# Other idle matmuls at the start, 144 empty instructions among the first products, and a set order of two rings, in a retention and gated feed-forward kernel

## The chip, the cores and the metric

The kernel runs on one core of a Trainium2 chip. The time is that of the device in microseconds (us); the time of an execution is a little longer than the span that the profile shows, since the span reaches only from the first instruction of the program to the last. PE is TensorE's matmul, PEld its weight load, DVE VectorE, ACT ScalarE, POOL GpSimd, SP SyncE, which issues nearly all transfers.

## The reference

```python
# q, k, v: (8, 8, 576, 64); moe_w_gate, moe_w_val: (512, 1536); moe_w_out: (1536, 512)
scores = np.matmul(q, k.transpose(0, 1, 3, 2)) / np.sqrt(D)
gamma = 1.0 - 2.0 ** (-5.0 - np.arange(H))
rel = pos[:, None] - pos[None, :]
Dmat = np.where(rel >= 0, gamma[:, None, None] ** rel, 0.0)
attn = np.matmul(scores * Dmat, v)                       # (8, 8, 576, 64)
x = attn.transpose(0, 2, 1, 3).reshape(4608, 512)
gate = 1.0 / (1.0 + np.exp(-(x @ moe_w_gate)))
out = (gate * (x @ moe_w_val)) @ moe_w_out               # (4608, 512)
```

Inputs and output are float32; the kernel multiplies in bfloat16 and adds up in float32.

## The kernel before

The decay is folded into tables: q and k are multiplied by powers of gamma while they are cast to bfloat16 (`cast_pair`, `cast_qk`). What an earlier piece of a sequence leaves for later ones goes through a running state of 64x64 per head. The 4608 rows of x are worked in columns of a transposed x (`xT`): a lead block of 512, two blocks of 256 (512 and 768), and seven blocks of 512 from 1024 on, whose products use a scheme of seven quarter products in place of eight (`quarter_units`, `quarters`).

The schedule is manual: each engine runs its instructions in the order in which the code issues them, and a wait is set where an instruction needs another's result or its buffer.

The lead part, in the order of PE's queue:

- idle matmuls on a zeroed tile `blank` (L245, ten of 128x512 by `fill_wide`), while the first loads of k and q land;
- for two pairs of row tiles: transposes of k and q (`pair_t`, L454), scores (`pair_qk`, L473), state (`first_st`, L510), the masked scores times v (`pair_intra`, L561), with a few idle matmuls among them (`fill`, `fill_wide`; two `fill_wide(2)` among the first scores and another ahead of the first gate product);
- the gate and value products of the lead block, 512 columns wide: column blocks 0 and 1 by `h_one` (hg, hv, L1263; with `pair_st` of one pair behind the first hv and one behind the second hg), 2 to 7 in twos by `h_two` (L1278), 8 to 11 by `h_both` (L1246). Gate tiles take the ring `qk_psum`, value tiles the ring `ffn_psum`; ACT applies the sigmoid, DVE multiplies. 96 matmuls;
- the out products of the lead block (`op_first`, L1426), 48 matmuls, mixed with the third pair of row tiles.

Then the main loop over `BLOCKS` begins. The two blocks of 256 take `h_units` (L816: h_g, h_v, two column blocks to a bank, DVE multiplies at L821) and `op_units` (L1156), whose out product number nb is put into bank nb of `ffn_psum`. Among these run the steps of the attention: `turn_step` (PE transposes for steps 0, 1 and 7, L591; the other steps' tiles are turned by DMA), scores and products into row tiles (L629, L637), values (L655, L670).

A `Ring` is a list of banks in the order in which they were last taken. A tile without a bank of its own takes the first in the list that is not held, and its bank goes to the end. A row tile of the ring of three always takes bank 2. When the main loop begins, the last takers of `ffn_psum` were op_0_0 (bank 1), op_0_1 (bank 2) and op_0_2 (bank 0), so its list is 1, 2, 0; that of `qk_psum`, where op_0_3 took bank 1 last, is 0, 1. In block 512 the order of `h_units` is h_g, h_v for column blocks 0, 2, 4, 6, 8, 10: twelve tiles.

`space()` puts an empty instruction (`nc.tensor.nop`, L252) into PE's queue as long as the list `owed` says so. Two of the later blocks use it:

```python
SPACES = {2560: 40, 3072: 40}
owed.extend([True, False, False, False] * SPACES.get(t0, 0))
```

PE is one instruction queue: each matmul is issued with a weight load of its own.

Of the kernel before, what the change touches and what calls it, by code (L numbers as in the profile page):

```python
# [16 lines left out]
def kernel(  # L17
# [70 lines left out]
    qk_psum = Ring(qk_banks, 2)  # L88
    ffn_psum = Ring(ffn_banks, 3)
# [140 lines left out]
    def idle_bank():  # L230
        idle.append(ffn_psum.tile([P, 4, P], FP32, tag="ffn", name=f"idle_{len(idle)}"))
# [3 lines left out]
    def fill(n, weights=P, columns=P):  # L235

        for i in range(n):
            nc.tensor.matmul(idle[-1][:weights, 0, :columns], lhsT=blank[:, :weights], rhs=blank[:, :columns], start=True, stop=True)

    def fill_wide(n):  # L240

        for _ in range(n):
            nc.tensor.matmul(idle[-1], lhsT=blank, rhs=blank.unsqueeze(1).to_broadcast([P, 4, P]), start=True, stop=True)

    fill_wide(10)  # L245

    SPACES = {2560: 40, 3072: 40}
    owed = []

    def space():  # L250
        if owed and owed.pop():
            nc.tensor.nop(hint="space")  # L252
# [119 lines left out]
    def xT(rows_, cols):  # L372

        t0, n = max(b for b in [(0, 512)] + BLOCKS if b[0] <= cols.start)
        assert cols.stop <= t0 + n
        if t0 not in x_tiles:
            x_tiles[t0] = x_pool.tile([P, M, 512], BF16, tag="x", name=f"xT_{t0}")
        return x_tiles[t0][:, rows_, cols.start - t0:cols.stop - t0]
# [22 lines left out]
    def cast_pair(nm, A, g, eng):  # L401

        if (nm, A) not in natural:
            natural[nm, A] = osb.tile([P, 2, H, D], BF16, tag="osb", name=f"{nm}p_{A}")
        if nm != "v" and A == 2:
            o = natural[nm, A].rearrange("p r (m y) d -> p y m r d", y=2)[:, g]
        else:
            o = natural[nm, A][:, :, g * M:(g + 1) * M, :].rearrange("p r h d -> p h r d")
        i = parts.pop((nm, "pair", A, g))
        if nm == "v":  # L410
            eng(out=o, in_=i)
        else:
            tab = (ktab2 if nm == "k" else qtab2)[:, PAIRS[A][1], g * M:(g + 1) * M, :].unsqueeze(3).to_broadcast([P, M, 2, D])
            eng.tensor_tensor(out=o, in0=i, in1=tab, op=ALU.mult)
# [409 lines left out]
    def gv_unit(t0, u):  # L824

        return gv_pool.tile([P, 4, 512], BF16, tag="gv", name=f"gv_{t0}_{u}")
# [3 lines left out]
    def gv_tile(gvs, t0, fc):  # L830

        if fc not in gvs:
            unit = made[t0, fc // 4] = gv_unit(t0, fc // 4)
            for i in range(4):
                gvs[fc // 4 * 4 + i] = unit[:, i]
        return gvs[fc]
# [63 lines left out]
    def quarter_units(gvs, t0):  # L900
# [44 lines left out]
        of = {}  # L945
        owed.extend([True, False, False, False] * SPACES.get(t0, 0))

# [282 lines left out]
    def last_step(t1):  # L1230
        return max(s for s in range(NS) if at_col[s] < t1)
# [3 lines left out]
    def turn(nm, A, g, pool=ffn_psum, tag="ffn"):  # L1235
        pair_t(nm, A, g, pool, tag, on_act)

    def h_both(fcs):

        for what in ("g", "v"):  # L1240
            for fc in fcs:
                gv = gv_tile(gvs, 0, fc)
                pool, tag = (qk_psum, "qk") if what == "g" else (ffn_psum, "ffn")
                ps = pool.tile([P, 512], FP32, tag=tag, name=f"h{what}_0_{fc}")
                for kc in range(NKC):
                    nc.tensor.matmul(ps, lhsT=(wg_sb if what == "g" else wv_sb)[:, kc, fc * P:(fc + 1) * P],  # L1246
                                     rhs=xT(kc, slice(0, 4 * P)), start=(kc == 0), stop=(kc == NKC - 1))
                if what == "g":
                    nc.scalar.activation(out=gv, in_=ps, func=AF.Sigmoid)
                else:  # L1250
                    nc.vector.tensor_tensor(out=gv, in0=gv, in1=ps, op=ALU.mult)
                yield
# [5 lines left out]
    def h_one(what, fc):  # L1258

        pool, tag = (qk_psum, "qk") if what == "g" else (ffn_psum, "ffn")  # L1260
        ps = pool.tile([P, 512], FP32, tag=tag, name=f"h{what}_0_{fc}")
        for kc in range(NKC):
            nc.tensor.matmul(ps, lhsT=(wg_sb if what == "g" else wv_sb)[:, kc, fc * P:(fc + 1) * P],  # L1263
                             rhs=xT(kc, slice(0, 4 * P)), start=(kc == 0), stop=(kc == NKC - 1))
        gv = gv_tile(gvs, 0, fc)
        if what == "g":
            nc.scalar.activation(out=gv, in_=ps, func=AF.Sigmoid)
        else:
            nc.vector.tensor_tensor(out=gv, in0=gv, in1=ps, op=ALU.mult)

    def h_two(what, f):

        pool, tag = (qk_psum, "qk") if what == "g" else (ffn_psum, "ffn")
        ps = [pool.tile([P, 512], FP32, tag=tag, name=f"h{what}_0_{f + j}") for j in range(2)]
        for i in range(2):
            for j in range(2):
                for kc in (2 * i, 2 * i + 1):
                    nc.tensor.matmul(ps[j], lhsT=(wg_sb if what == "g" else wv_sb)[:, kc, (f + j) * P:(f + j + 1) * P],  # L1278
                                     rhs=xT(kc, slice(0, 4 * P)), start=(kc == 0), stop=(kc == NKC - 1))
        for j in range(2):  # L1280
            gv = gv_tile(gvs, 0, f + j)
            if what == "g":
                nc.scalar.activation(out=gv, in_=ps[j], func=AF.Sigmoid)
            else:
                nc.vector.tensor_tensor(out=gv, in0=gv, in1=ps[j], op=ALU.mult)
# [22 lines left out]
    cast_pair("q", 0, 0, nc.vector)  # L1308
    turn("k", 0, 0, *TR)
    turn("q", 0, 0, *PV)  # L1310
    fill_wide(2)
    cast_pair("q", 0, 1, nc.vector)
    pair_qk(0, 0, QK)
    turn("k", 0, 1, *TR)
    fill(3)
    turn("q", 0, 1, *PV)
    fill_wide(2)
    cast_pair("q", 1, 0, nc.vector)
    pair_qk(0, 1, FF)
    turn("k", 1, 0, *TR)  # L1320
# [34 lines left out]
    pair_out(1, 1, on_act, on_dve)  # L1355
    idle_bank()
    fill_wide(2)
    h_one("g", 0)
    h_one("v", 0)
    pair_st(0, ST)  # L1360
    h_one("g", 1)
    pair_st(1, TR)
    h_one("v", 1)
# [59 lines left out]
    def op_first(fcs, nbs, opps):  # L1423
        for fc in fcs:
            for nb in nbs:
                nc.tensor.matmul(opps[nb], lhsT=gvs[fc][:, nb * P:(nb + 1) * P], rhs=wo_sb[:, fc, :],  # L1426
                                 start=(fc == 0), stop=(fc == NFC - 1))

    opps = [ffn_psum.tile([P, 512], FP32, tag="ffn", name=f"op_0_{nb}") for nb in range(3)]
    op_first((0, 1), range(2), opps)  # L1430
# [59 lines left out]
    pieces = 0  # L1490
    slots = 0
    valued = -1
    for w, (t0, n) in enumerate(BLOCKS):
        nxt = BLOCKS[w + 1] if w + 1 < len(BLOCKS) else None
        last = last_step(nxt[0] + nxt[1]) if nxt else NS - 1
        early = list(EARLY[w]) if w < len(EARLY) else []
        n_h = NFC if n <= 256 else 2 * NFC
        if n == 512:
            n_h = 0
        twos = []  # L1500
        at = slots
        while not early and (not twos and valued < last or twos and twos[-1][0][-1] < last):
            vals = list(range((twos[-1][0][-1] if twos else valued) + 1, at))
            twos.append((vals, list(range(at, min(at + 2, NS)))))
            at = min(at + 2, NS)
        for i, cols in enumerate(ffn_units(t0, n, nxt)):
            if i in SUMS_AT.get(w, ()) and weight_sums:
                weight_sums.pop(0)()
            for step, turn_at in TURN_AT:
                if turn_at == (w, i):  # L1510
                    turn_step(step)
            for x in SPARE.get((w, i - n_h if w == 1 else i), ()):
                x()
            pieces += 1
            if w == 2 and i in (24, 32):
                keeps[0] -= 1
                leave()
            if stores and (nxt is None or w + 2 == len(BLOCKS) and pieces % 4 == 0):
                leave()
            if n > 256 and i % 2 and i < n_h:  # L1520
                continue
            if pending:
                pending.pop(0)()
            elif early:
                if i >= early[0][0]:
                    _, vals, news = early.pop(0)
                    next_two(vals, news, False)
                    valued, slots = ([valued] + vals)[-1], news[-1] + 1
            elif twos and cue:
                cue.clear()  # L1530
                next_two(*twos[0], True)
                valued = twos[0][0][-1]
                slots = max([slots] + [s + 1 for s in twos.pop(0)[1]])
        assert not twos and not early
        while pending:
            pending.pop(0)()
# [31 lines left out]
```

## Time and profile before

| | |
|---|---|
| median of 3 runs | 308.21 us (307.74 to 308.53) |
| the profiled execution | 308.12 us, span 306.4 us |
| PE, PEld busy | 296.4 us (97%), 238.6 us (78%) |
| DVE, POOL, ACT busy | 244.9 us, 209.2 us, 194.9 us |
| PE instructions | 4427 matmuls, 4427 weight loads, 80 empty ones |
| lead block of 512 (to about 54 us), blocks 512 and 768 (to 93.0 us) | 54 us, 39 us |
| a block of 512 from 1024 on | 30.2 us |

In a row of the waits stand who waited and for whom, the sum in us, how often, and the longest. A row of the chain in order of time has start, length and what ran; "issue" is time for which the profile shows no cause. A row of the timeline has start, length, engine, line, operation, out<-in, shape and count, and in brackets the idle time of the engine before it with what ended it; the matmuls of a row overlap, so its length is that of the last one's modelled end. A row of a stretch has its limits and length, then for PE, PEld, DVE, ACT and POOL the busy us and, in brackets, the number of instructions, then the clock granted to PE, the DMA share and GB/s.

### The profile page before, as it was taken

The page shows a single profiled execution, that of the slowest core. Times are in us where ns is not written, and L with a number is a line of the kernel's source. Part 1 is how long each engine was busy: PE and PEld are TensorE (multiplying, and loading weights), DVE is VectorE, ACT ScalarE, POOL GpSimd, SP SyncE. Part 2 cuts the span into 40 slices and gives each one's busy share as a digit, 9 for nine tenths or more (in the row PEclk, how much of TensorE's full clock was granted, in tenths as well). Part 3 has the DMA queues.
Part 4 walks back from the last instruction along what each step waited for, and adds up shares of the span by engine and source line. Part 5 has one row for each costly group of instructions (what it writes and reads, how often), then busy time and mean ns, then how long its engine had stood idle before and what let it go on. Part 6 is the DMA issues. An engine that isn't in the chain of part 4 may idle for free.

```text
span 306.4 us, 10818 instructions
## 1 busy us (share of the span) xinstructions
PE 296.4 (97%) x4427; PEld 238.6 (78%) x4427; DVE 244.9 (80%) x464; ACT 194.9 (64%) x414; POOL 209.2 (68%) x256
## 2 busy tenths in 40 slices
PE   7889999989999999999999999999999999999994
PEld 3644445866868888888888888888888888888883
DVE  5837877887898899689978997898789968945793
ACT  6634744425548757874897479757965886648640
POOL 5875653644467689869976997699769916751670
PEclk9999999999999999999999999999999999999999
DMA  7999999799999992998899948992980390012004
GB/s 208 343 373 403 347 284 214 178 194 193 195 209 213 243 242 52 230 262 181 169 189 226 183 97 204 219 211 63 189 221 4 93 250 8 2 57 84 2 2 137
DMA packets 145730, 54.98 MB, mean 179 GB/s; under 512 B 124048, under 2 KB 138640, under 8 KB 145680
## 3 DMA queue, kind: packets, MB, share of 16 engines
q1 hardware_dynamic: 144880, 53.63, 73.2%
q8 instruction: 35, 0.57, 0.8%
q10 hardware_dynamic: 800, 0.66, 0.7%
q14 instruction: 15, 0.12, 0.1%
HBM read 37.75 MB, written 9.44 MB: 154 GB/s over the span
## 4 chain that ended last, share of the span: by engine, by line
PE 88%; DVE 5%; issue 2%; ACT 2%; DMA 1%; POOL 0%; SPq 0%; DVEq 0%
PE gatea L940 12%; PE wa L940 12%; PE qa L1054 11%; PE qe L1054 9%; PE gatee L940 6%; PE we L940 6%; PE gateg L940 3%; PE op L1156 3%; PE wg L940 3%; PE op L1426 3%; PE h_v L816 2%; PE h_g L816 2%; PE val L655 2%; PE hv L1278 2%; PE hg L1278 2%
## 5 line engine op out<-in xcount | busy, mean ns | idle before, releaser
L427 POOL TENSOR_TENSOR qk<-k,ktab 128x512 bf16<-128x512 f32 x30 | 32.0, 1067 | 9.5 <-DMA k<-in_k_dram 8.0
L1054 PEld LDWEIGHTS <-gsum 128*128 128x128 bf16 x336 | 31.9, 98 | 5.0 <-DVE gsum L877 0.8
L877 POOL TENSOR_TENSOR gsum<-gv 128x256 bf16<-128x256 bf16 (+1 forms) x35 | 26.5, 765 | 13.2 <-DVE gv L965 12.0
L427 POOL TENSOR_TENSOR qk<-q,qtab 128x512 bf16<-128x512 f32 x28 | 30.9, 1102 | 3.6 <-DMA q<-in_q_dram 3.6
L940 PEld LDWEIGHTS <-wg_sb 128*128 128x128 bf16 x308 | 30.1, 98 | 3.7
L940 PEld LDWEIGHTS <-wv_sb 128*128 128x128 bf16 x308 | 30.1, 98 | 3.5
L940 PEld LDWEIGHTS <-wvt 128*128 128x128 bf16 x280 | 27.4, 98 | 3.3
L940 PEld LDWEIGHTS <-wgt_sb 128*128 128x128 bf16 x252 | 24.7, 98 | 2.9
L965 POOL TENSOR_TENSOR gv<-gv,wu 128x512 bf16<-128x512 bf16 x7 | 8.1, 1162 | 26.4 <-DVE wu L991 26.4
L877 POOL TENSOR_TENSOR gsum<-gv,gsum 128x256 bf16<-128x256 bf16 x37 | 25.4, 716 | 0.0
L1054 PEld LDWEIGHTS <-gv 128*128 128x128 bf16 x240 | 23.0, 98 | 3.0
L644 DVE TENSOR_TENSOR pt<-row,tri 128x256 bf16<-128x256 f32 x60 | 21.2, 412 | 4.0 <-PE row L637 3.4
L715 ACT CAST xT<-val 128x256 bf16<-128x256 f32 x60 | 18.9, 388 | 5.9 <-PE val L670 5.9
L432 POOL CAST v<-v 128x512 bf16<-128x512 f32 x20 | 13.7, 683 | 11.9 <-DMA v<-in_v_dram 10.1
L606 ACT CAST sb<-s 128x256 bf16<-128x256 f32 x46 | 17.9, 416 | 5.3 <-DVE s L742 3.1
L940 PE MATMUL wa<-xsum,wv_sb 128*128 128x256 bf16 x140 | 21.0, 273 | 0.0
L940 PE MATMUL gatea<-xsum,wg_sb 128*128 128x256 bf16 x140 | 19.9, 273 | 0.0
L965 POOL TENSOR_TENSOR gv<-gv,ws 128x512 bf16<-128x512 bf16 x15 | 17.5, 1165 | 2.9 <-DVE ws L994 2.9
L994 DVE TENSOR_TENSOR gs<-gatea,gs 128x512 f32<-128x512 f32 x21 | 13.9, 688 | 6.0 <-PE gatea L940 5.2
L994 DVE TENSOR_TENSOR ws<-wa,ws 128x512 f32<-128x512 f32 x21 | 14.4, 685 | 4.2 <-PE wa L940 4.1
L963 ACT ACTIVATE gv<-gs 128x512 bf16<-128x512 f32 x21 | 13.0, 630 | 7.0 <-DVE gs L994 7.0
L986 DVE TENSOR_TENSOR gatee<-gatea,gs 128x512 f32<-128x512 f32 x14 | 9.8, 699 | 9.0 <-PE gatea L940 6.3
(191 smaller groups left out, 857.3 us busy)
## 6 DMA issues: line engine op xcount, KB each, us to landing
k<-in_k_dram SPq DMA_DIRECT2D x26, 256.0 KB, 4.3
q<-in_q_dram SPq DMA_DIRECT2D x26, 256.0 KB, 4.4
v<-in_v_dram SPq DMA_DIRECT2D x26, 256.0 KB, 4.3
out_dram<-ob SPq DMA_DIRECT2D x25, 256.0 KB, 3.1
wg<-in_moe_w_gate_dram SPq DMA_DIRECT2D x12, 256.0 KB, 5.4
wv<-in_moe_w_val_dram SPq DMA_DIRECT2D x12, 256.0 KB, 5.4
wo<-in_moe_w_out_dram SPq DMA_DIRECT2D x12, 256.0 KB, 5.1
v32p<-in_v_dram SPq DMA_DIRECT2D x6, 256.0 KB, 4.5
```

What stands on the lines that cost most here:

```text
L427: eng.tensor_tensor(out=natural_qk[s][:, i].rearrange("p m (y d) -> p y m d", y=2), in0=by_halves(loaded[s][1 - i]), in1=tab, op=ALU.mult)
L432: eng(out=natural["v", s], in_=loaded[s][2])
L606: eng(out=state[key], in_=src)
L644: nc.vector.tensor_tensor(out=probs[s][:, y], in0=row_ps[s][y][:, 0], in1=tri.unsqueeze(1).to_broadcast([P, M, 64]), op=ALU.mult)
L715: nc.scalar.copy(out=x_out(ALL, cols_of(s, i)), in_=x_in(val_ps[s][i], cols_of(s, i)))
L816: nc.tensor.matmul(ps[:, i], lhsT=w_sb[:, kc, (fc + i) * P:(fc + i + 1) * P], rhs=xT(kc, slice(t0, t0 + n)), start=(kc == 0), stop=(kc == ...
L877: eng.tensor_tensor(out=to, in0=a, in1=b, op=op)
L940: nc.tensor.matmul(ps[:, f], lhsT=w[:, kc, f * P:(f + 1) * P], rhs=x[:, kc], start=(first and f == 0 and kc == 0), stop=(f == 1 and kc == ...
L963: nc.scalar.activation(out=to, in_=src, func=AF.Sigmoid)
L965: eng.tensor_tensor(out=to, in0=to, in1=src, op=ALU.mult)
L994: nc.vector.tensor_tensor(out=me["s5"], in0=a, in1=me["s5"], op=ALU.add)
L1054: nc.tensor.matmul(ps[:, b], lhsT=left(fp)[:, b * P:(b + 1) * P], rhs=right(fp), start=(first and fp == 0 and b == 0), stop=(fp == NFC // ...
```

## The change

The ten wide idle matmuls at the start become 56 of 64 columns, and the two `fill_wide(2)` among the first scores become seven of 128 columns each. Counted with their weight loads, these are 112 instructions more, all ahead of the masked scores. `owed` gets 144 entries ahead of the first `h_one`, and `space()` is called behind each matmul of `h_one`, `h_two`, `h_both` and `op_first`: 144 empty instructions, one for each of these 96 and 48 matmuls. Ahead of the main loop both rings are given an order: 0, 1, 2 for `ffn_psum` and 1, 0 for `qk_psum`.

```diff
-    fill_wide(10)
+    fill(56, columns=64)

     SPACES = {2560: 40, 3072: 40}
+    SPACES_FIRST = 144
...
                 for kc in range(NKC):
                     nc.tensor.matmul(ps, lhsT=(wg_sb if what == "g" else wv_sb)[:, kc, fc * P:(fc + 1) * P],
                                      rhs=xT(kc, slice(0, 4 * P)), start=(kc == 0), stop=(kc == NKC - 1))
+                    space()
...
     turn("q", 0, 0, *PV)
-    fill_wide(2)
+    fill(7)
     cast_pair("q", 0, 1, nc.vector)
...
     turn("q", 0, 1, *PV)
-    fill_wide(2)
+    fill(7)
     cast_pair("q", 1, 0, nc.vector)
...
     idle_bank()
     fill_wide(2)
+    owed.extend([True] * SPACES_FIRST)
     h_one("g", 0)
...
                 nc.tensor.matmul(opps[nb], lhsT=gvs[fc][:, nb * P:(nb + 1) * P], rhs=wo_sb[:, fc, :],
                                  start=(fc == 0), stop=(fc == NFC - 1))
+                space()
...
     valued = -1
+    ffn_psum.order = [0, 1, 2]
+    qk_psum.order = [1, 0]
     for w, (t0, n) in enumerate(BLOCKS):
```

The same `space()` stands in `h_one` and `h_two`. `fill(n, weights, columns)` issues n matmuls of `blank` by `blank` with that many columns into an idle bank; `fill_wide(n)` issues n of 512 columns.

More of the change, by code (lines that the diff above doesn't have):

```diff
@@ L1279, in h_two @@
                                      rhs=xT(kc, slice(0, 4 * P)), start=(kc == 0), stop=(kc == NKC - 1))
+                    space()
         for j in range(2):
@@ L1427, in op_first @@
                                  start=(fc == 0), stop=(fc == NFC - 1))
+                space()
     opps = [ffn_psum.tile([P, 512], FP32, tag="ffn", name=f"op_0_{nb}") for nb in range(3)]
```

## The prediction

> **What bounds the kernel now.** I read the page's head, then who waited for whom on PE, then the chain in order of time, and last the counts of instructions in single stretches.
>
> ```profile
> span 306.4 us, 10818 instructions
> PE 296.4 (97%) x4427; PEld 238.6 (78%) x4427; DVE 244.9 (80%) x464; ACT 194.9 (64%) x414; POOL 209.2 (68%) x256
> q8 instruction: 35, 0.57, 0.8%
> PE 88%; DVE 5%; issue 2%; ACT 2%; DMA 1%; POOL 0%; SPq 0%; DVEq 0%
> ```
> ```profile
> PE qkp L473 <- ACT qT L464: 1.3, 4, 0.4
> PE pvp L561 <- issue: 1.1, 1, 1.1
> PE op L1156 <- DVE gv L821: 0.8, 1, 0.8
> ```
>
> TensorE bounds the kernel: 97% busy, 88% of the chain. So a change that leaves the matrix products alone can gain only where PE stands still. Two single waits are large: 1.1 us at L561 for which the profile names no releaser, and 0.8 us at L1156 for a gate-value product on DVE. The rest of PE's waits are at the start, for ACT, DVE and POOL, and no wait of PE is for a DMA. The line of queue q8 is the clue to the first wait: 0.57 MB in 35 packets is 16.3 KB each, and PE's 8,854 shown instructions and 80 empty ones over 35 packets are 255 apiece. So q8 brings PE's own code in blocks of (I take) 256.
>
> **The first wait, and the 112 instructions ahead of it.** The chain, then the counts:
>
> ```profile
> 15.00 0.19 PE pvp L561 x11
> 15.19 1.11 issue
> 16.30 0.41 PE pvp L561 x8
> 17.67 1.02 PE hg L1263 x4
> 20.90 0.37 PE st_None L497 x16
> 21.27 0.97 PE hv L1263 x4
> 22.24 1.73 PE hg L1278 x8
> ```
> ```profile
> 0.00:7.70 7.70, 5.83 (x43) 2.55 (x43) 4.04 (x22) 4.77 (x10) 4.25 (x14) 1.00 0.73 208
> 0.00:11.33 11.33, 8.55 (x96) 4.45 (x96) 7.01 (x26) 7.56 (x14) 7.43 (x17) 1.00 0.86 252
> 0.00:13.82 13.82, 10.69 (x167) 6.21 (x168) 8.89 (x29) 8.85 (x17) 9.59 (x21) 1.00 0.91 269
> 0.00:15.10 15.10, 11.97 (x223) 7.45 (x223) 10.17 (x31) 9.32 (x18) 10.70 (x22) 1.00 0.93 275
> 16.29:21.19 4.90, 4.78 (x66) 2.35 (x66) 1.75 (x3) 1.22 (x3) 4.20 (x9) 1.00 1.09 381
> ```
>
> The wait lies inside one run of equal matmuls (x11, then x8) whose operands and bank the first of them had already, so nothing but the next instruction can be missing. It comes after 223 weight loads and 223 matmuls, 446 instructions. Read as a block's end, the end before is at 446 - 256 = 190, which PE passes at 11.33 (96 + 96). If passing one end asks for the block behind the next, the code took from 11.33 to 16.30: 5.0 us.
>
> Every matmul stands with its own weight load. 56 narrow idle matmuls for 10 wide ones add 92 instructions, twice 7 for 2 add 20: 112, all ahead of both points. So block ends move back by 112. The first falls after 334 old instructions (13.82; 167 + 168), the one before at 190 - 102 = 88 (7.7, 43 + 43; the last 10 of the 112 are not yet passed there). Code asked for at 7.7 is there at 12.7 by the 5.0 us, and needed at 13.8: no wait, 1.1 us to spare. That takes 1.11 off. The next thing late would be the operands of hg and hv, and they are in time: the weights that POOL casts last for the four single products are ready at 17.78, and hv that uses them comes at 21.27 - 1.1 = 20.2.
>
> ```profile
> 17.17 0.61 POOL L311 CAST wv_sb<-wv 128x512 bf16<-128x512 f32 x1
> ```
>
> **The empty instructions and the new second end.** One empty instruction stands behind each of the 96 first gate and value matmuls and the 48 first out products: 144. Before hv of the second column block, the old count is 446 + 132 (the stretch 16.29 to 21.19) = 578. New it is 578 + 112 + 12 empty = 702 = 446 + 256. So the second block end falls exactly ahead of the hv at 21.27, now 20.2. Its code is asked for at 13.82. By 5.0 us it is there at 18.8, 1.4 before need. But DMA moves 381 GB/s there against 275 before, and if a fetch stretches with that, 5.0 x 381 / 275 = 6.9 us: there at 20.7, 0.5 late. I take 0.25, between the two; the ends are 0 and 1.1 (a wait that gives the whole gain back). From there on PE streams 512-wide products, 256 instructions of which (with a third of them empty) last over 18 us, so no later end can be late in this part. And 112 + 144 is 256: behind the last first out product, every block end lies where it lies now, so the rest of the program should neither gain nor lose by it.
>
> What an empty instruction costs can be read from the blocks that have 40 of them already, the third and fourth of these stretches:
>
> ```profile
> L252 PEldq NOP  x80: 13/13/13, 183.2 to 230.0; - x80
> ```
> ```profile
> 93.00:123.19 30.19, 30.19 (x490) 26.74 (x489) 26.64 (x50) 21.41 (x46) 24.46 (x29) 1.00 0.81 185
> 153.51:183.80 30.29, 30.29 (x507) 26.91 (x505) 26.26 (x50) 22.66 (x50) 25.27 (x30) 1.00 0.84 176
> 183.80:213.96 30.16, 30.16 (x490) 26.73 (x489) 25.74 (x48) 22.53 (x49) 25.19 (x30) 1.00 0.86 176
> 213.96:244.18 30.22, 30.22 (x506) 26.92 (x505) 26.38 (x50) 22.82 (x50) 25.30 (x30) 1.00 0.54 117
> ```
>
> Stretches of 490 matmuls: 30.19 without, 30.16 with. Of 506 and 507: 30.22 with, 30.29 without. So 0 us for one in four 256-wide matmuls. Here it is one for each, but each matmul is 512 wide and lasts 0.216 us (1.73 / 8), against 13 ns on the sequencer. I take 0; the other end is 144 x 13 ns = 1.9 us, if nothing covered them.
>
> **The idle matmuls themselves.**
>
> ```profile
> 1.05 3.65 PE L243 MATMUL idle<-blank 128*128 128x512 bf16 x10 [1.05 <-DVE blank L226]
> 4.78 0.40 PE L454 MATMUL kTp<-ident,kp 128*128 128x128 bf16 x4
> 11.33 0.40 PE L238 MATMUL idle<-blank 128*128 128x128 bf16 x4
> ```
> ```profile
> 3.16 0.15 PEld L243 LDWEIGHTS <-blank 128*128 128x128 bf16 x1 [0.28 <-issue]
> 3.59 0.15 PEld L243 LDWEIGHTS <-blank 128*128 128x128 bf16 x1 [0.27 <-issue]
> ```
>
> A wide one takes 0.43 us up to 3.59, so by width a 64-wide one takes 0.054, and 56 take 3.0: done at 4.1, ahead of the first transpose at 4.78. The other bound is the weight load: four 128-wide ones last 0.40 with a fixed part of some 0.2, or 0.06 each later on, hence 0.12 at the early pace; 22 up to 3.7 and 34 at 0.06 end at 5.7, and delay the first transpose by 0.9. Taken: 0, since the width sets the pace in the nearest row. The two sevens are 7 x 0.06 = 0.4 us for 2 x 0.216 = 0.43, under the waits for ACT qT: 0.
>
> **The rings.** Now the ring of three stands at 1, 2, 0 when the main loop begins, and the twelve products of block 512 take the banks in turn, so the last value product sits in bank 0, which the first out product names. It must wait until DVE has read it:
>
> ```profile
> 64.77 0.68 DVE L821 TENSOR_TENSOR gv<-gv,h_v 128x512 bf16<-128x512 bf16 x1
> 65.97 0.69 DVE L821 TENSOR_TENSOR gv<-gv,h_v 128x512 bf16<-128x512 bf16 x1 [0.51 <-PE h_v L816]
> 91.41 0.42 DVE L742 TENSOR_TENSOR s<-s,row 128x256 f32<-128x256 f32 x1
> ```
> ```profile
> 66.70 1.89 PE L1156 MATMUL op<-wo_sb,gv 128*128 128x512 bf16 x8 [0.85 <-DVE gv L821]
> 69.92 3.63 PE L1156 MATMUL op<-wo_sb,gv 128*128 128x512 bf16 x16
> ```
> ```profile
> 93.00 0.87 PE gatea L940 x8
> ```
>
> Starting at 0, 1, 2 the last one sits in bank 2, and bank 0 holds the value product before the last but one, read by 65.45. So the out product starts behind the h_v before it: 0.85 less. What is late next: columns 10 and 11 of the same out product need the value written by 66.66, and they come in the group of 16 at 69.92 - 0.85; the row tile in bank 2 comes with the scores just ahead of that group. Both have over 2 us. The ring is back in the old order after the second out product. The ring of two only swaps the two row tiles, and the first to notice is the second gate product behind 93.00, whose bank is then read until 91.83 instead of some 0.4 sooner: still 1.6 us early. Bounds 0 and 0.85; I take 0.85, since PE has no other wait until the end that a shift brings nearer: loads and casts are ahead of it.
>
> ```profile
> 80.37 1.04 POOL L427 TENSOR_TENSOR qk<-q,qtab 128x512 bf16<-128x512 f32 x1 [0.54 <-DMA q<-in_q_dram]
> ```
> ```profile
> 85.83 0.61 PE L591 MATMUL turn<-ident,qk 128*128 128x128 bf16 x8
> ```
>
> This cast, the nearest that I found, is done 4.4 us before PE turns its tile, more than the two gains together.
>
> **Sum.** -1.11 + 0.25 - 0.85 = -1.7 us. The profiled execution took 308.12 us around its span of 306.4, so 306.4, and its time lies 0.09 under the median of the runs shown (308.21). Forecast: 306.5.
>
> **Rivals.**
> (1) The wait moves: the code for the second end, asked for in the busiest stretch of DMA, comes a microsecond late, so that only the ring's 0.85 is left: 307.4. For it speaks the 381 GB/s, against it the 1.4 us to spare by the one fetch that can be timed.
> (2) The 1.11 us is not code, so it stays, whatever is ahead of it: 307.4 as well. Against it: equal matmuls on both sides, and no releaser. [...]
> (3) The ring's wait comes back at the next DVE step, so only the 0.85 is lost as a gain: 307.3 with my 0.25, 307.0 without.
> (4) Slower: the empty instructions keep weight loads from running ahead. A weight load is 0.098 us here, under a 0.216 us product; exposed behind each of the 144 it would be 14 us, 320. It decides from 12 ns each (1.7 / 144) against any gain, from 18 ns (2.6 / 144) as a loss beyond 0.9 us. Against it stand the two blocks with 40.
>
> ```profile
> L940 PEld LDWEIGHTS <-wg_sb 128*128 128x128 bf16 x308 | 30.1, 98 | 3.7
> ```
>
> **How the numbers follow.** About 0.3% (0.9 us) is what a measurement here can tell from no change, so faster is under 307.3. Forecast 0.57 (306.1 to 307.0); (1) 0.15, (2) 0.06, (3) 0.10, (4) 0.07, and 0.05 for the idle matmuls ending late or rousing PE less, up to 309. Faster: 0.57, 0.09 of (3) and 0.03 of (1): 0.69. Slower: (4) and 0.02: 0.09. Same: 0.22. The range reaches down to the full 1.96 with 0.4 of scatter, up past (1) and (2): 305.9 to 307.7.
>
> **What would show it.** Right: no gap of 1.1 us among the L561 products; hg of the first block near 16.6 instead of 17.67; hv of the second without an "issue" gap over 0.3 ahead of it; eight hg L1278 still 1.73; the L1156 wait gone; q8 with 36 packets; blocks from 93 on as long as now, each about 1.7 earlier. Wrong: an "issue" gap that has only moved to another place of the first 21 us; 512-wide products over 0.216; or the first transposes later than 4.8.

## The result, and the profile after

Over ten runs each the changed kernel took 306.72 us (305.45 to 307.5) and the kernel before 308.25 (307.33 to 311.05): ratio 0.9938 [0.991, 0.9966]. On another chip it was 307.22 against 308.28, ratio 0.9957 [0.9933, 0.9981]. The gain is some 1.1 to 1.5 us. The profiled execution of the changed kernel took 306.89 us, its span is 1.2 us shorter than before.

The head of the page after, with the share of the chain by engine last:

```profile
span 305.2 us, 11063 instructions
PE 296.5 (97%) x4473; PEld 242.7 (80%) x4483; DVE 240.1 (79%) x464; ACT 195.0 (64%) x414; POOL 208.4 (68%) x256
q8 instruction: 36, 0.59, 0.8%
PE 93%; ACT 2%; DVE 1%; issue 1%; POOL 0%; ACTq 0%; POOLq 0%
```

PE's busy time is the same (the trace has no record of 10 of its 4,483 matmuls), its share of the chain went from 88% to 93%: PE waits less. Of PE's waits behind its first matmul these are the largest for an engine and the largest without a releaser (columns: who waited and for whom, us in all, how often, the longest):

```profile
PE kTp L455 <- POOL kp L415: 0.7, 1, 0.7
PE row L638 <- issue: 0.3, 1, 0.3
```

The 1.1 us at the masked scores (now L562) and the 0.8 us at the first out product of block 512 (now L1157) are gone. The chain in order of time, at the places that the prediction named:

```profile
15.69 0.22 PE pvp L562 x8
15.92 0.42 PE pvp L562 x19
...
17.30 0.38 PE hg L1265
...
20.53 0.37 PE st_None L498 x16
20.91 0.97 PE hv L1265 x4
...
23.60 1.73 PE hv L1281 x8
...
65.16 0.35 PE op L1157
...
91.08 0.87 PE gatea L941 x8
...
202.79 0.28 issue
```

The masked scores run through. That the wait before was for code can be seen in the packed trace (the records of which the views are made), which has the time of each packet of q8: the packet of that block ended at 14.88, and PE went on 1.42 us later, at 16.30. After, the packets of the first two blocks ended at 10.98 and 17.18, and PE came to the two ends only at 14.75 and 20.91. The hv at the new second block end (20.91) starts where the state products end (20.53 + 0.37), so nothing waits there. Eight products with an empty instruction behind each still take 1.73 us. But the first hg starts at 17.30, not near 16.6: only 0.37 earlier than before. What went against it stands in the timeline of the start:

```profile
1.05 3.17 PE L238 MATMUL idle<-blank 128*128 128x64 bf16 x56 [1.05 <-DVE blank L226]
4.89 0.61 PE L455 MATMUL kTp<-ident,kp 128*128 128x128 bf16 x4 [0.67 <-POOL kp L415]
5.84 0.95 PE L238 MATMUL idle<-blank 128*128 128x128 bf16 x7
7.59 0.61 PE L455 MATMUL kTp<-ident,kp 128*128 128x128 bf16 x4
10.20 0.40 PE L455 MATMUL kTp<-ident,kp 128*128 128x128 bf16 x4
12.26 0.40 PE L238 MATMUL idle<-blank 128*128 128x128 bf16 x4
41.29 0.39 PE L455 MATMUL qTp<-ident,qp 128*128 128x128 bf16 x4
```

The 56 narrow matmuls end at 4.2, as the width said, and nothing is late because of that: the first transposes start at 4.89, behind the 4.8 that the prediction named as a sign of being wrong, but they wait for POOL's cast. But four transposes take 0.61 us at 4.89 and again at 7.59, and 0.40 only from 10.20 on; before, they took 0.40 from 4.78 on. PE runs at its slow pace some 6 us longer. The four idle matmuls that stood at 11.33 start at 12.26, 0.93 later. (The granted clock in the rows of stretches reads 1.00 for the start in both traces. The packed trace tells more: its record of full clock begins at 3.76 us before and at 9.98 after, where the pace of equal work changes too.)

Against that stand two places at which the trace after is ahead though no part of the change aimed at them. The trace before has these rows, the first in the timeline, the second in the chain:

```profile
41.98 0.40 PE L454 MATMUL qTp<-ident,qp 128*128 128x128 bf16 x4 [0.16 <-DVE qp L414]
88.06 0.34 DVE T L593
```

There PE waited for DVE's cast of q at 41.98 and for DVE's copy of turned tiles at 88.06, and lost some 0.3 us at each. In the trace after DVE is in time at both. That is no gain of the change: the first wait, 0.16 again, is also in the traces of the rings alone and of the 40 empty instructions (below), and not in most of the others; the second is in none of the other thirteen traces, those included that stand behind at 88 us. So it belongs to the one execution before that was profiled.

The lead over the trace before, added up along PE's queue: 0.37 at the first hg (1.11 less 0.74 that the slower start costs), 0.69 at the transposes of q (41.98 to 41.29), 1.54 at the first out product of block 512 (66.70 to 65.16), 1.92 at the first gate product of the main blocks (93.00 to 91.08), and 1.2 at the end. So 0.7 us is given back behind 93 us. Most of that goes at one place, shown here by the timeline before and then after:

```profile
204.21 0.32 PE L637 MATMUL row<-v,qk 64*64 64x64 bf16 x16
204.59 1.48 PE L1054 MATMUL qe<-wo_sb,gv 128*128 128x256 bf16 x12
```
```profile
202.54 0.25 PE L638 MATMUL row<-v,qk 64*64 64x64 bf16 x6
203.41 1.48 PE L1055 MATMUL qe<-wo_sb,gv 128*128 128x256 bf16 x12
```

The lead is 1.67 at the row products and 1.18 behind them, with the issue wait of 202.79 between. That wait stands behind 3,073 weight loads, as many matmuls and 184 empty instructions, 6,330: 5,884 behind the 446 of the first wait, four short of 23 times 256. The code packet ended at 201.59, 1.48 before PE went on at 203.07. So it is a block's end.

### The profile page after: what moved, and what is told of

The parts are those of the page before. It is cut to its first block, busy times and chain, and to the rows that moved or that the text cites. A ratio compares the mean times of both kernels' runs of the same rounds, so it can differ in the third digit from the quotient of the medians.

```text
span 305.2 us, 11063 instructions
## 1 busy us (share of the span) xinstructions
PE 296.5 (97%) x4473; PEld 242.7 (80%) x4483; DVE 240.1 (79%) x464; ACT 195.0 (64%) x414; POOL 208.4 (68%) x256
## 4 chain that ended last, share of the span: by engine, by line
PE 93%; ACT 2%; DVE 1%; issue 1%; POOL 0%; ACTq 0%; POOLq 0%
PE gatea L941 12%; PE wa L941 12%; PE qa L1055 11%; PE qe L1055 9%; PE gatee L941 6%; PE we L941 6%; PE h_v L817 4%; PE h_g L817 3%; PE op L1157 3%; PE op L1431 3%; PE gateg L941 3%; PE wg L941 3%; PE val L656 2%; PE hv L1281 2%; PE hg L1281 2%; PE row L630 2%
## 5 line engine op out<-in xcount | busy, mean ns | idle before, releaser
L428 POOL TENSOR_TENSOR qk<-q,qtab 128x512 bf16<-128x512 f32 x28 | 30.0, 1073 | 4.2 <-DMA q<-in_q_dram 4.2
```

What stands on the lines that cost most here:

```text
L428: eng.tensor_tensor(out=natural_qk[s][:, i].rearrange("p m (y d) -> p y m d", y=2), in0=by_halves(loaded[s][1 - i]), in1=tab, op=ALU.mult)
```

## The experiments

The theory after the result: T1, the 1.11 us was PE's code, and the instructions ahead cured it; T2, the ring order gave its 0.85; T3, the narrow idle matmuls cost 0.7 to 0.9 through the clock; T4, the 144 cost nothing. Each kernel ran beside the kernel before. Ratios are to it.

**The rings alone**, in the kernel before:

```diff
+    ffn_psum.order = [0, 1, 2]
+    qk_psum.order = [1, 0]
```

> The kernel before with the new order of the two rings and nothing else. If the wait at the first out product of block 512 is for bank 0: that wait (0.85 us) goes, the 1.1 us gap in the lead part stays, the first hg stays at 17.7, the time falls by 0.9 to 1.2 us (the trace of the changed kernel has some 0.4 more between 75 and 90, where DVE leads). If the wait only comes back at the next DVE step: no change.

Measured: 307.37 us (306.31 to 308.19) against 308.14, ratio 0.9979 [0.9962, 0.9997], span 305.6. The waits no longer hold the first out product of block 512. They still hold this, at the old place:

```profile
PE pvp L561 <- issue: 0.5, 1, 0.5
```

The chain has the first gate product of the main blocks at 91.27 (93.00 before), though the span is only 0.8 shorter. Of that lead 0.5 goes at a wait for DVE:

```profile
105.60 0.60 PE L940 MATMUL gatee<-xsum,wgt_sb 128*128 128x256 bf16 x4 [0.36 <-DVE gv L965]
```

So the ring order is worth 0.8 us by itself in the medians, as T2 has it, and does not touch the other wait, whose size varies from one execution to another (1.1 and 0.5). Here PE came to the block's end at 15.48, 0.29 later than before, and the packet had ended at 14.71; PE went on at 16.03, 1.32 later.

**All but the rings**: the changed kernel without these two lines.

> The changed kernel without the order of the rings. Theory: the lead part gains 0.4 us up to the first hg (1.1 from the code wait, less 0.7 for a slow clock) and 0.3 more by the out products, so 0.3 to 0.8 us less than before, and the 0.85 us wait at the first out product of block 512 is back. Rival: the lead part's gain is lost behind it, no change.

Measured: 308.03 us (306.54 to 309.41), ratio 0.9988 [0.9964, 1.0012], span 307.5. The wait at the out product is back, and here the clock came later still:

```profile
PE kTp L455 <- POOL kp L415: 1.7, 2, 1.0
PE op L1157 <- DVE gv L822: 0.8, 1, 0.8
```
```profile
11.24 0.61 PE L455 MATMUL kTp<-ident,kp 128*128 128x128 bf16 x4
```

Four transposes still take 0.61 at 11.24. So the idle matmuls and the empty ones together, whose part of the forecast was -1.11 + 0.25, bring nothing that can be told from zero. In this trace what the code wait gave went into a later start, the slow pace and POOL's casts together. That fits T3 and does not show it: the profiled execution (309.22) is among the longer ones of this kernel.

**Wide idle matmuls again, with empty instructions in place of the narrow ones**, so that all counts stay as in the changed kernel:

```diff
-    fill(56, columns=64)
+    for _ in range(10):
+        fill_wide(1)
+        for _ in range(9):
+            nc.tensor.nop(hint="space")
+    for _ in range(2):
+        nc.tensor.nop(hint="space")
...
-    fill(7)
+    fill_wide(2)
+    for _ in range(10):
+        nc.tensor.nop(hint="space")
```

(The last twice, for both groups of seven.)

> The changed kernel with the wide idle matmuls of before, and 112 empty instructions in place of the narrow matmuls, so that every code block ends where it ends in the changed kernel. Theory (narrow idle matmuls do not raise PE's clock in time): four transposes take 0.40 us from the start on as before, not 0.61; the first hg starts at 16.6 instead of 17.3; 0.5 to 0.8 us less than the changed kernel. Rival (the clock's rise is a matter of chance, whatever the idle matmuls): 0.40 or 0.61 by chance, same time as the changed kernel on average. Rival 2 (112 empty ones cost more than they hide): the wide matmuls are stretched beyond 4.7.

Measured: 309.18 us (308.89 to 309.93), ratio 1.0038 [1.0016, 1.0059], so slower than before. The timeline of the start, then of the weight loads:

```profile
1.05 6.69 PE L243 MATMUL idle<-blank 128*128 128x512 bf16 x10 [1.05 <-DVE blank L226]
7.96 0.58 PE L460 MATMUL kTp<-ident,kp 128*128 128x128 bf16 x4 [0.21 <-issue]
1.70 0.11 PEld L243 LDWEIGHTS <-blank 128*128 128x128 bf16 x1 [0.55 <-issue]
```

With nine empties between them the wide ones start 0.65 us apart instead of 0.43, ten take 6.69 us, and the first transposes move from 4.78 to 7.96. Nine empties and two instructions in 0.65 us are some 0.06 us each on average, not the 13 ns that the profile shows for one. So the run did not isolate the width: it made a new bound, and idle work with gaps in it did not raise the clock by 7.96 either (0.58 for four). As a test of the width it is a miss.

**40 empty instructions behind the ten wide idle matmuls, nothing else**, in the kernel before:

```diff
     fill_wide(10)
+    for _ in range(40):
+        nc.tensor.nop(hint="space")
```

> The kernel before with 40 empty instructions behind the ten wide idle matmuls and nothing else. If the 1.1 us gap is a block of code that is late: the gap begins 40 instructions earlier, after 203 weight loads and 203 matmuls instead of 223 each, and is 0.3 to 1.1 us long. If it belongs to the matmul at L561: it stays behind 223 and 223.

Measured in one run: 306.79 us, span 305.1. The wait at the out product stays (0.8). The timeline and the chain:

```profile
1.05 4.45 PE L243 MATMUL idle<-blank 128*128 128x512 bf16 x10 [1.05 <-DVE blank L226]
```
```profile
15.16 0.42 PE pvp L563 x19
16.55 0.59 PE hg L1265 x2
```

No issue wait is left among the masked scores, and hg starts at 16.55, which is the 1.1 us that the prediction wanted. That is neither of the two things expected: the gap has not moved 40 instructions forward, it is gone. An empty instruction takes 13 ns in the trace before, waits for nothing there and nothing waits for it; what the 40 change is the place in the code at which the blocks end. The block's packet ended at 12.25 here, 2.6 us sooner than before, and PE came to that end at 14.75. That speaks against the rival by which the wait is not code; the next run settles it.

**8 empty instructions at the same place.**

```diff
     fill_wide(10)
+    for _ in range(8):
+        nc.tensor.nop(hint="space")
```

> The kernel before with 8 empty instructions behind the ten wide idle matmuls and nothing else. If the 1.1 us gap is a late block of code: it begins 8 instructions earlier, after 219 weight loads and 219 matmuls, 0.4 to 1.1 us long (40 of them made it go, since the fetch is asked for sooner too). If it belongs to the matmul at L561: it stays behind 223 and 223, or is gone.

Measured in one run: 308.15 us, span 306.4. The waits, and the stretch from the start to where PE stands:

```profile
PE val L657 <- issue: 0.5, 1, 0.5
PE pvp L563 <- issue: 0.3, 1, 0.3
```
```profile
0.00:15.98 15.98, 13.09 (x219) 8.10 (x219) 10.29 (x31) 9.52 (x19) 10.67 (x22) 1.00 0.92 265
```

219 matmuls and 219 loads, 438, and the 8 empties are 446: the count at which the wait stood before (223 and 223). So it moved by four matmuls in the work, as a block's end does. It also shrank to 0.3; a second one of 0.5 came in the first of the seven main blocks, 11 times 256 instructions (less two) behind the first. The place follows from the count. The size does not follow from eight instructions by the prediction's 5.0 us. It follows from the packet: that ended at 14.78 here, much as in the trace before (14.88) and with the rings alone (14.71), and PE went on 1.3 to 1.5 us after it in all three (16.23, 16.30, 16.03), but came to the end later, at 15.98, and so waited less. The same holds for all seven such waits of 0.25 us or more in these traces: PE goes on 1.31 to 1.48 us behind the end of a packet on q8. That leaves nothing of the rival.

**The changed kernel without the 144.**

```diff
-    SPACES_FIRST = 144
+    SPACES_FIRST = 0
```

> The changed kernel without the 144 empty instructions among the first products: code blocks end 112 instructions earlier than before through the whole program. If the 144 matter by what they bring back into place: new gaps after 60 us, 0.5 us or more above the changed kernel. If they neither cost nor bring anything: the same time as the changed kernel within 0.3 us.

Measured: 309.89 us (307.87 to 311.06), ratio 1.0055 [1.0035, 1.0076]: 1.6 us over the kernel before, where the changed kernel lies 1.1 to 1.5 under it. So the 144 are worth some 3 us. The chain has two large waits without a releaser:

```profile
117.72 0.16 PE row L630 x16
117.88 0.11 PE val L671 x13
117.99 0.89 issue
149.97 1.22 issue
```

And the stretch from the end of the first to the start of the second, with the stretch behind it, up to the next gap, a small one:

```profile
118.87:149.97 31.10, 31.09 (x512) 27.42 (x512) 25.10 (x49) 22.18 (x50) 25.19 (x30) 1.00 0.91 205
151.18:182.37 31.19, 31.18 (x511) 27.64 (x512) 25.87 (x49) 22.28 (x50) 24.87 (x29) 1.00 0.88 171
```

512 weight loads and 512 matmuls are 1,024 instructions, four times 256, in both stretches (one matmul of the second has no record). This is the plainest sight of code blocks in these traces. The two packets ended at 117.57 and 149.78, and PE went on at 118.88 and 151.19. Without the 144, all ends of the main loop stand 112 instructions earlier in the work, and two of them fall into or just behind a run of short matmuls (16 in 0.16 us), where PE comes to the end sooner than the next block does. The 144 bring the shift to 256 and the ends to where they were.

**80 narrow idle matmuls in place of 56**, in the changed kernel:

```diff
-    fill(56, columns=64)
+    fill(80, columns=64)
```

> The changed kernel with 80 narrow idle matmuls at the start instead of 56, so that they last as long as the ten wide ones (about 4.3 us instead of 3.2). If PE's clock stays low because the narrow ones end too early: four transposes take 0.40 us from the first or second group on, and the first hg starts at 16.6 to 17.0. If it stays low because they are narrow: 0.61 us for the first four groups as in the changed kernel, first hg at 17.3 or later.

Measured in one run: 305.95 us, span 304.2.

```profile
1.05 4.45 PE L238 MATMUL idle<-blank 128*128 128x64 bf16 x80 [1.05 <-DVE blank L226]
5.31 0.61 PE L455 MATMUL kTp<-ident,kp 128*128 128x128 bf16 x4
7.66 0.40 PE L455 MATMUL kTp<-ident,kp 128*128 128x128 bf16 x4
```

The second group of transposes is fast at 7.66, where it was slow at 7.59 with 56. The width is the same, so the width alone did not keep the clock low: with 4.45 us of narrow idle matmuls full clock is on record from 6.04 us, with the 3.17 us of the changed kernel from 9.98. The first hg is hardly earlier, though (17.26): later transposes of k now wait 0.8 for POOL's cast.

**80 narrow and 96 empty ones**, 256 in all again (48 + 112 + 96), so that the main loop's blocks end where they did:

```diff
-    SPACES_FIRST = 144
+    SPACES_FIRST = 96
...
-    fill(56, columns=64)
+    fill(80, columns=64)
```

> The changed kernel with 80 narrow idle matmuls instead of 56 and 96 empty instructions among the first products instead of 144: the same 256 in all. Theory (56 end too early to raise the clock, 80 do not): the first transposes of the second group take 0.40 us, first hg at 16.9 to 17.3, 0.5 to 0.9 us less than the changed kernel. Rival (narrow matmuls do not raise it, the one look at 80 was chance): the clock rises near 10 us and the time is that of the changed kernel.

Measured: 307.16 us (305.97 to 309.86), ratio 0.9977 [0.9948, 1.0007]. The transposes are fast at once:

```profile
5.26 0.39 PE L455 MATMUL kTp<-ident,kp 128*128 128x128 bf16 x4
```

and the profiled execution has a span of 304.4 against 305.4 for the changed kernel on that chip, hg at 17.05 against 17.45. But the runs scatter over 3.9 us, and the median is that of the changed kernel (307.22). The longer executions are those with the lower granted clock: 0.987 to 0.991 in the five above 307.8 us, 0.996 or more in the other seven; what lowers it there is not shown. So the earlier clock is shown, a gain in time from 80 narrow ones is not.

**Wide idle matmuls, 40 empties behind them, 216 among the first products** (1 and 2 in turn), rings as in the changed kernel:

```diff
-    fill(56, columns=64)
+    fill_wide(10)
+    for _ in range(40):
+        nc.tensor.nop(hint="space")
...
-        if owed and owed.pop():
+        for _ in range(owed.pop() if owed else 0):
...
-    fill(7)        # twice
+    fill_wide(2)
...
-    owed.extend([True] * SPACES_FIRST)
+    owed.extend([1, 2] * (SPACES_FIRST // 2))
```

> The changed kernel with the wide idle matmuls of before, 40 empty instructions behind the first ten, and 216 instead of 144 among the first products (two behind every other one): 256 in all, so later code blocks end where they end before. Theory (the gain of the changed kernel was cut by the slow clock): first hg at 16.6, no wait at the first out product of block 512, 2.0 to 2.4 us less than before, 0.5 to 0.9 less than the changed kernel. Rival (a slow clock costs nothing, the lead part's end is set elsewhere): same as the changed kernel. If the second empty one shows: eight hg of the lead block take more than 1.73 us.

Measured: 306.07 us (305.82 to 307.09) against 308.28, ratio 0.994 [0.9919, 0.996], span 304.3.

```profile
16.74 1.02 PE hg L1267 x4
```
```profile
23.04 1.73 PE hv L1283 x8
```

The first hg starts at 16.74, and eight products with one or two empties behind each take 1.73 us: the empties are covered there. Against the changed kernel the intervals overlap.

**40 empties behind the wide ones and the ring order, no more**: the edits of the first and the fourth experiment together, run on two chips.

> The kernel before with the 40 empty instructions behind the ten wide idle matmuls and the new order of the rings; no empty ones among the first products, so that all later code blocks end 40 instructions earlier than before. If where they end does not matter later on: the same time as the version with 256, 2.0 to 2.4 us less than before. If it does: 0.3 us or more above it, with gaps in the stretches of short matmuls after 100 us.

> The kernel with 40 empty instructions behind the ten wide idle matmuls and the new order of the rings once more, beside the changed kernel: 0.8 to 1.4 us less than the changed one, clock rising before 6.1 us.

Measured: 305.41 us (305.05 to 306.15) against 308.28, ratio 0.9919 [0.9894, 0.9944], span 303.5; and 305.88 (305.59 to 306.57) against 308.28, ratio 0.9914 [0.9887, 0.9941], span 303.9. The start in the first of them, by the timeline, and two places of its chain:

```profile
1.05 3.80 PE L243 MATMUL idle<-blank 128*128 128x512 bf16 x10 [1.05 <-DVE blank L226]
4.85 0.40 PE L456 MATMUL kTp<-ident,kp 128*128 128x128 bf16 x4
```
```profile
16.37 1.02 PE hg L1265 x4
90.13 0.87 PE gatea L942 x8
```

It is the fastest kernel of the study: on the same chip 305.88 against the changed kernel's 307.22, and of the lead that it has at 93 us (2.9 in the first run, 2.7 in the second) it keeps 2.9 and 2.5 to the end. A shift of the later ends by 40 cost little or nothing, one of 112 some 3 us, and one of 8, in its single run, a wait of 0.5.

**The changed kernel once more**, beside the last three on one chip:

> The changed kernel once more, on the chip of the other runs of this call: 1.5 us less than before, clock rising after 9 us (the first four groups of transposes at 0.61 us).

Measured: 307.22 us (306.49 to 308.63) against 308.28, ratio 0.9957 [0.9933, 0.9981], span 305.4; slow transposes again (0.61 at 5.04 and 7.59), hg at 17.45. That is 1.1 us less than before, not the 1.5 expected. The interval overlaps slightly with that of the fastest kernel, though of the runs only the lowest one (306.49) lies within the other's range.

## Why the prediction came out, and where it did not hold

The forecast was 306.5, the median 306.72. Step by step, in the traces:

- The code wait, -1.11: right, and for the stated reason. It goes with 40 empty instructions alone (hg 16.55), it moves with 8, without the 144 such waits stand exactly 1,024 instructions apart, and each of the seven such waits ends 1.31 to 1.48 us behind a code packet. The rival by which it isn't code falls. Two of the seven, those without the 144, lasted 0.89 and 1.22 us.
- The wait at the second end, +0.25: nothing there. PE was only 0.37 early there, not 1.1, but that did not decide it: the block's packet ended at 17.18, 2.4 us behind the first end (14.75), and with 1.5 us more, which is what PE took behind a packet at most, the code was there at 18.7, 2.2 before 20.91. So the fetch did not stretch to 6.9 us. That passing one end asks for the block behind the next, from which the 5.0 us come, was the author's assumption and is not shown: in the trace before, the packet in question starts on q8 at 13.93, 2.60 behind the passing at 11.33, and ends at 14.88.
- The 144 empty instructions, 0: right (1.73 for eight products). What they are for the prediction saw only in part: it noted that 112 + 144 is 256 and that the later ends stay, but gave no price for a shift of the ends without them. It is some 3 us.
- The idle matmuls, 0: this step failed. The bounds, 0 and 0.9, were for the time at which the 56 are done, and that came by width as taken (4.2). The cost came from the clock, which the prediction had only as a few words in the last 0.05 of its chances: "rousing PE less". The two sevens, priced at 0.4 us by the fast pace, took 0.95 each. Measured: 0.93 at the idle matmuls of 12.26, 0.74 left at the first hg. The traces bear that size out in part: without a code wait hg starts at 16.37 to 16.85 with the wide ones set without gaps and at 17.18 to 18.55 with 56 narrow ones, but at 17.05 and 17.26 with 80, whose clock is early and where transposes of k wait 0.8 in all for POOL's casts. What the slow pace costs the whole kernel no run shows by itself. The profile before held the sign for it: ten wide ones of 3.65 us and transposes at 0.40 right behind them, so the fast pace had begun by then; a cut of the idle work to 3.0 us should have raised the question of whether it still would.
- The rings, -0.85: right (-0.85 between the transposes of q and the out product, -0.8 alone).
- No other wait of PE shifts: not so in the two traces, but the change is not shown to be the cause. DVE's two late tiles at 41.98 and 88.06 are in time in the trace after, 0.32 and 0.38 more, by the luck of the executions that were profiled, as said above. Behind 93 us the lead shrinks by 0.72, of which 0.49 goes at the block's end near 203 us. The trace before and the kernel with 256 empties pass that same end of a block without loss, the rings alone lose 0.2 there, and with the ends 40 instructions elsewhere nothing is lost at this place. So an end that stays where it lay can still cost something in one execution and nothing in another. The other 0.2 is spread over the main blocks and was not taken apart.

Sum in the profile: -1.11 + 0.74 - 0.32 - 0.85 - 0.38 + 0.72 = -1.20, against the forecast's -1.71. The 0.74 lost at the start was made up by the 0.70 of DVE's two tiles, and the 0.72 given back in part by the 0.25 that was never due. These are single executions; the medians differ by 1.53 and, on the other chip, by 1.06. The two large terms were right in place and size. That the total came so close is luck: a cost that was left out stood against others with the opposite sign.

Of the signs that the prediction named for being right, hg near 16.6 and every block from 93 on 1.7 earlier failed (17.30; 1.9 falling to 1.2), the others came. The other rivals: the ring's wait did not come back (no DVE wait of PE in block 512), and the weight loads run ahead as before in spite of the empties (1.73 us for eight products, as before).

## What to carry to other kernels

A wait with no releaser inside a run of equal matmuls is worth counting instructions for. Here two waits without a releaser stood 1,024 instructions apart, four times 256, and at all seven of 0.25 us or more PE went on 1.31 to 1.48 us behind the end of a packet on q8, the instruction queue: signs of code. 40 empty instructions behind the ten wide idle matmuls moved the end away from there, and the wait of 1.1 us went; then look at every later end, since all of them move (a shift by 112 cost some 3 us). The start of full clock went with the time that idle matmuls lasted without gaps (by 6.55 us behind 3.65 to 4.45 us of them, not before 9.18 behind 3.17), not with their number (10 and 80 on the one side, 56 on the other), so read the pace of equal work behind them before shortening them. And when a bank is named by number, look at who took it last: here two lines of order took a wait of 0.85 us away.

## What the runs showed of the hardware

- The clock. The packed traces have a record of full clock (granted clock 1.00). It begins at 3.76 to 6.55 us in the nine traces with ten wide or 80 narrow idle matmuls, which last 3.65 to 4.45 us without gaps, at 9.18 to 12.62 in the four with 56 narrow ones of 3.17 us, and at 11.13 in the one with gaps in 6.69 us of idle work. The pace agrees: four transposes take 0.40 us by 8.0 us at the latest in the nine, and still 0.61 at 7.55 or later in the four. From there full clock lasts 293.55, 296.96, 300.37 or 303.79 us, 3.41 or 3.42 apart; no run shows why. Nor is it shown how much idle work is enough: before, full clock began 2.71 us behind PE's first matmul (3.76 less 1.05), and 3.17 us of narrow ones did not bring it that early in any of the four traces.
- An empty instruction on PE's queue is shown as 13 ns and cost nothing behind 512-wide products, one or two in turn (1.73 us for eight, as without); with nine behind each wide idle matmul these start 0.65 us apart instead of 0.43.
- The ends of code blocks. In the trace before 35 packets on q8 stand against 8,934 instructions of PE, 255 apiece. Where short matmuls run up to an end PE waited 0.3 to 1.2 us at seven places (0.28 to 1.22); at the ends that lie behind 512-wide products in the lead block (34.2 us before, 20.9 and 39.0 after) it did not wait. At all seven PE went on 1.31 to 1.48 us behind the end of the block's packet on q8 (16.30 behind 14.88 in the trace before).
